# Up projection of the second sweep as seven half-width block products per pair of tiles, with its operands reread from DRAM

## The chip, the cores and the metric

The kernel runs on one core of a Trainium2 chip. The metric is the device time of one execution in microseconds. Three runs of the kernel before took 506.97, 507.06 and 507.6 us, median 507.06. One execution was profiled as well. TensorE (PE) multiplies; its weight loads are listed apart as PEld. VectorE (DVE), ScalarE (ACT) and GpSimd (POOL) do the elementwise work, and SyncE (SP) issues nearly all DMA transfers, one after the other, from one queue that also waits in order.

## The reference

One input x of 2048 rows and 512 columns feeds two branches, mixed by a gate per row. Everything is float32.

```python
g = sigmoid((x * gate_w).sum(-1, keepdims=True))
# a: linear attention, 32 heads of 16; softmax features of q and k, both signs
q, k, v = split(x @ wqkv)
phi_q, phi_k = [concat(softmax(p), softmax(-p)) for p in (q @ w_phi, k @ w_phi)]
a = ((phi_q @ (phi_k.T @ v)) / (phi_q @ phi_k.sum() + 1e-6)) @ wo
# b: feed forward, 512 -> 1792 -> 512
h = x @ w1 + b1
b = where(h > 0, h, 0) ** 2 @ w2 + b2
out = g * a + (1 - g) * b
```

## The kernel before

Every product is made from two parts of each operand, a high part (a copy rounded to the matmul's input type) and a low part (the rest): high by high, high by low, low by high. `mm3` (L73) issues these three matmuls for one pair of 128-row operands.

The feed forward is worked in two sweeps. A sweep takes seven of the fourteen tiles of 128 hidden columns; inside a sweep the loop runs over four row blocks of 512 rows of x, and inside a row block over the seven tiles. For one tile, *up* (L471) makes a bank of 128 hidden columns by 512 rows in 12 matmuls of 512 columns. ACT applies bias and relu, squares, and copies out the high part; DVE subtracts for the low part (`hidden`, L457 on). Two tiles later *down* (L486) multiplies the tile by w2 into four PSUM banks (d0 to d3, called down columns here), three matmuls of 512 columns each. The main loop (L761 on) counts these tiles as t; each t has two *steps* (2t and 2t+1), and a table filled by `at(slot, ...)` (L670) says which other work is issued in which step. The first sweep also makes keys and values and sums them up. The second sweep begins at t = 28 (step 56) and carries the query side: per 128 rows a q projection (`do_q`, 12 matmuls), the feature work on DVE, ACT and POOL, a transpose on DVE (tb), and twelve small DMAs that move its 32 x 256 blocks into phiT (`transposed`, L403). Per pair of such row chunks come the numerators (`numer`, L419, 32 small matmuls) and two applications of wo (`finish`, att). phiT has one buffer, so the transfers of a pair of chunks wait for the numerators of the pair before.

In the second sweep w1 and w2 stay in SBUF: the seven tiles of each are loaded and split once around its begin (L728 to L731), three of each in a ring (`fpool`) and four in slots of `wpool` that the first sweep no longer needs (L94). x is read back per row block, high and low parts, from a DRAM copy that the first sweep made (`x_save`, `load_x`). The up banks come from a pool of two (`ps_u`). The order of instructions on each engine is set by a scheduler from the order of the code, priorities and explicit `issue_after` ties; each engine then works its row in order.

```python
work_list = [(sw, b, i) for sw in range(2) for b in range(NB) for i in range(NFH)]
for nm, s in (("w1", 48 + 2 * i if i < NSTR else 47 + 2 * i), ("w2", 52 + 2 * i)):
```

Of the kernel before, what the change touches and what calls it, by code (L numbers as in the profile page):

```python
# [16 lines left out]
P = 128  # L17
# [14 lines left out]
FOLD_AT = 9, 3  # L32
KEPT_LATE = ("w1", 0), ("w1", 1), ("w2", 0)
SUMS = ("t1", "t2", "t15", "k2")


@with_exitstack
def tile_gated_mix(ctx: ExitStack, tc: tile.TileContext, xT, xn, wqT, wkT, wphi, wv, wo, w1, b1, w2, b2, gw, out):
# [34 lines left out]
    def mm3(o, a, b, sa, sb, first, last, **kw):  # L73
        (ah, al), (bh, bl) = a, b
        nc.tensor.matmul(o, ah[:, sa], bh[:, sb], start=first, stop=False, **kw)  # L75
        nc.tensor.matmul(o, ah[:, sa], bl[:, sb], start=False, stop=False, **kw)  # L76
        return nc.tensor.matmul(o, al[:, sa], bh[:, sb], start=False, stop=last, **kw)  # L77

    ALL = slice(0, 512)
    halves = (slice(0, 256), slice(256, 512))  # L80

# [54 lines left out]
    def x_tiles(b, k):  # L136
        return (xpool.tile([P, SB], F32R, tag="xh", name=f"xh{b}_{k}"),
                xpool.tile([P, SB], F32R, tag="xl", name=f"xl{b}_{k}"))


    def x_save(b):
# [4 lines left out]
    def load_x(b):  # L146
        xs = []
        for k in range(NK):
            xs.append(x_tiles(b, k))
            for j in range(2):  # L150
                nc.sync.dma_start(xs[k][j].bitcast(F32), xkept[b, k, j])
        return xs


    def x_fetch(b):
# [27 lines left out]
    zrow = dram.tile([2 * D], F32, name="zrow")  # L183
    xkept = dram.tile([NB, NK, 2, P, SB], F32, name="xkept")
    lkept = dram.tile([NFH, 2, P, 512], F32, name="lkept")
    kvs = const.tile([P, 2 * P], F32, name="kvs")
    nc.gpsimd.memset(kvs, 0.0)
    vext = [hold.tile([P, H * VW + 32 - VW], F32, tag="vz", name=f"vext{i}") for i in range(NV)]
# [149 lines left out]
    def project(c, xs, ws, nm):  # L338
        ps = bank(nm)
        sc = slice(c * P, (c + 1) * P)  # L340
        for k in range(NK):
            mm3(ps, xs[k], ws[k], sc, ALL, k == 0, k == NK - 1)
        return ps

    def exps(ps, tag="e"):
# [73 lines left out]
    def numer(pt):  # L419
        pss = [bank(f"num{r}") for r in range(2)]  # L420

        def mm(t, q, r):
            rows = slice(64 * r, 64 * r + 64)
            return nc.tensor.matmul(pss[r][32 * q:32 * q + 32, t * 2 * P:(t + 1) * 2 * P], kvb[rows, 4 * t + q, :],
                                    pt[rows, :, :, 4 * t + q, :].rearrange("p u r s -> p (u r) s"),
                                    start=True, stop=True, skip_group_check=True)


        todo = [(t, q, r) for t in range(2) for q in range(4) for r in range(2)]
        first = mm(*todo[0])  # L430
        with tc.issue_after(first.ins):
            second = mm(*todo[1])
        with tc.issue_after(second.ins):
            for x in todo[2:]:
                mm(*x)
        o = []
        for r in range(2):
            oh = work.tile([P, 512], F32R, tag="oh", name="oh", bufs=2)
            ol = work.tile([P, 512], F32R, tag="ol", name="ol", bufs=2)
            with tc.high_priority(offset=AHEAD):  # L440
                split(pss[r], oh, ol, nc.scalar, nc.vector)
            o.append((oh, ol))
        return o

    def attended(o, u, wos):
        ps = bank("att")
        for r in range(2):
            for t in range(2):
                mm3(ps, o[r], wos[2 * r + t], slice((2 * t + u) * P, (2 * t + u + 1) * P), ALL,
                    r + t == 0, r + t == 2)  # L450
        return ps


    def up_step(ps, k, xs, wf):
        st["up"] = mm3(ps, wf, xs[k], slice(k * P, (k + 1) * P), ALL, k == 0, k == NK - 1)

    def hidden(fc, ps, later=False):  # L457
        r = work.tile([P, SB], F32, tag="r", name="r")
        nc.scalar.activation(r, ps, AF.Relu, bias=b1c[:, fc:fc + 1])  # L459
# [4 lines left out]
        low = lambda: st.update(low=nc.vector.tensor_tensor(hl, r, hh.bitcast(F32), ALU.subtract))  # L464
        if later:
            st["rest"] = low
        else:
            low()
        return hh, hl

    def up(fc, xs, wf, later):  # L471
        ps = ps_u.tile([P, SB], F32, tag="u", name="u")
        if fc == 1 and xs is st["x", 0]:

            kk = [slice(k * P, (k + 1) * P) for k in range(NK)]
            for k in range(NK):
                for j in range(2):
                    nc.tensor.matmul(ps, wf[0][:, kk[k]], xs[k][j], start=k + j == 0, stop=False)
            for k in range(NK):
                st["up"] = nc.tensor.matmul(ps, wf[1][:, kk[k]], xs[k][0], start=False, stop=k == NK - 1)  # L480
        else:
            for k in range(NK):
                up_step(ps, k, xs, wf)
        return hidden(fc, ps, later)

    def down(t, c, dps):  # L486
        sw, b, i = work_list[t]
        end = i == NFH - 1 or t == last - 2 and c == NC - 1
        st["down"] = mm3(dps[c], hid[t], down_w[sw * NFH + i], slice(c * P, (c + 1) * P), ALL, i == 0, end)

    def do_w(src):
        st["wb"] = load_w(src)
# [10 lines left out]
    def start():  # L503
# [38 lines left out]
            do_up(1)  # L542
        raw.pop(("w1", 0))
        fetch_v()

    def do_x(b):
        st["x", b] = load_x(b - NB)

    def product(ps, p, a, op, first, last):
        b, q = divmod(p, 2)  # L550
# [119 lines left out]
    def at(slot, f, *a):  # L670
        steps.setdefault(int(slot), []).append(lambda: f(*a))
# [40 lines left out]
    for b in range(NB):  # L712
        for c in range(NC):
            s = b * SL + 2 * c if b else 7 + c
            at(s, gate_load, b * NC + c)
            at(s + 2, gate_dot, b * NC + c)
        at(b * SL + 12, gates, b)
        at(b * SL + 15, x_save, b)
# [5 lines left out]
    at(46, foldq_fetch)  # L724
    for k in range(NK):
        at(50 + k, foldq_ready, k)
    at(base + 11, do_w, wo)
    for i in range(NFH):  # L728
        for nm, s in (("w1", 48 + 2 * i if i < NSTR else 47 + 2 * i), ("w2", 52 + 2 * i)):
            at(s - 2, fetch, nm, NFH + i)  # L730
            at(s, ready, nm, NFH + i)  # L731
    at(NB * SL - 1, kv_done)


# [1 line left out]
    for p in range(NB * NC // 2):  # L736
# [9 lines left out]
    for b, slot in enumerate((46, 63, 72, 82)):  # L746
        at(slot, do_x, NB + b)
# [13 lines left out]
    for t, (sw, b, i) in enumerate(work_list):  # L761
# [3 lines left out]


        with tc.issue_after(st["down"].ins) if 0 < t <= LAG else nullcontext():
            fold("k") if t == 1 else do_up(t + LAG)
        for f in steps.get(2 * t + 1, ()):
            f()  # L770
        if i == 0:
# [100 lines left out]
```

## Time and profile before

| | |
|---|---|
| median of three runs | 507.06 us |
| the profiled execution | 506.81 us |
| its span, first to last instruction | 505.0 us |
| mean granted TensorE clock | 1.000 |
| TensorE matmul busy | 500.7 us |
| weight loads / DVE / ACT / POOL busy | 404.0 / 405.2 / 253.9 / 75.6 us |
| DMA packets moved | 84.79 MB, mean 168 GB/s |

The span is 1.8 us shorter than the execution it belongs to. Busy time of PE is the time with a matmul under way; matmuls are pipelined, so the distance between starts is what one costs, and the listed length of one is longer than that. In a line of groups the columns are line, engine, operation, output and inputs, shapes and count, then busy us and mean ns of one, then idle time before and what ended it. In a timeline line they are start, length, engine, line, operation and count.

### The profile page before, as it was taken

What the parts mean: (1) busy time and instruction counts of PE and PEld (TensorE: products, weight loads), DVE (VectorE), ACT (ScalarE), POOL (GpSimd) and SP (SyncE); (2) the same over time, 40 slices, a digit from 0 to 9 for tenths busy, and PEclk for the clock granted to TensorE, in tenths of its full rate; (3) what the DMA queues carried; (4) which work ended last, traced back from release to release, by engine and by line L of the source; (5) the groups of instructions that cost most, each with busy time, mean ns of one, the idle gap of its engine ahead of it and who ended that gap; (6) DMA issues with size and microseconds to landing.
All of it is one profiled execution on the core that took longest, in us unless ns stands there. A gap on an engine that the chain in (4) does not pass through costs nothing.

```text
span 505.0 us, 9519 instructions
## 1 busy us (share of the span) xinstructions
PE 500.7 (99%) x3616; PEld 404.0 (80%) x3616; DVE 405.2 (80%) x642; ACT 253.9 (50%) x433; POOL 75.6 (15%) x77
## 2 busy tenths in 40 slices
PE   9999999999999999999999999999999999999997
PEld 4878887788888888888888878787887878788876
DVE  4979996898877868797889898968789677798724
ACT  6598573364743646373765653443425353433530
POOL 5304020302050000000004122202122222202100
PEclk9999999999999999999999999999999999999999
DMA  8998888965657656845669161212153321032102
GB/s 296 331 361 299 232 283 270 321 234 192 212 183 245 236 165 208 279 140 155 187 183 311 51 195 52 91 51 92 39 185 96 86 74 44 8 100 82 43 22 83
DMA packets 52437, 84.79 MB, mean 168 GB/s; under 512 B 8104, under 2 KB 14504, under 8 KB 52392
## 3 DMA queue, kind: packets, MB, share of 16 engines
q1 hardware_dynamic: 52072, 83.79, 51.5%
q8 instruction: 28, 0.46, 0.4%
q10 hardware_dynamic: 288, 0.39, 0.3%
q14 instruction: 17, 0.14, 0.1%
q0 software_dynamic: 32, 0.01, 0.0%
HBM read 56.37 MB, written 21.50 MB: 154 GB/s over the span
## 4 chain that ended last, share of the span: by engine, by line
PE 97%; ACT 1%; DMA 1%; DVE 0%; issue 0%
PE d L75 10%; PE u L75 10%; PE d L77 10%; PE d L76 10%; PE u L76 10%; PE u L77 10%; PE q L75 3%; PE q L77 3%; PE att L77 3%; PE q L76 3%; PE att L76 3%; PE att L75 3%; PE ky L75 2%; PE ky L76 2%; PE ky L77 2%; PE kvps L378 2%
## 5 line engine op out<-in xcount | busy, mean ns | idle before, releaser
L459 ACT ACTIVATE r<-u,b1c 128x512 f32<-128x512 f32 x56 | 38.4, 685 | 146.1 <-PE u L77 146.0
L387 POOL TENSOR_TENSOR ez<-e,z 128x512 f32<-128x512 f32 x32 | 41.3, 1312 | 279.8 <-ACT e L358 160.5
L75 PE MATMUL d<-w2h,hh 128*128 128x512 f32 x160 | 62.7, 392 | 0.0
L77 PE MATMUL d<-w2h,hl 128*128 128x512 f32 x160 | 62.3, 389 | 0.0
L76 PE MATMUL d<-w2l,hh 128*128 128x512 f32 x160 | 62.3, 389 | 0.0
L75 PE MATMUL u<-xh,w1h 128*128 128x512 f32 x152 | 59.6, 392 | 0.1
L76 PE MATMUL u<-xl,w1h 128*128 128x512 f32 x152 | 59.2, 389 | 0.0
L77 PE MATMUL u<-xh,w1l 128*128 128x512 f32 x152 | 59.2, 389 | 0.0
L363 DVE TENSOR_REDUCE sm<-e 128x64 f32<-128x1024 f32 x32 | 38.9, 1215 | 18.5 <-ACT e L358 18.5
L464 DVE TENSOR_TENSOR hl<-r,hh 128x512 fp32r<-128x512 f32 x56 | 38.5, 687 | 13.8 <-ACT hh L463 13.7
L411 ACT ACTIVATE phiT<-tb 32x256 f32<-32x256 f32 x64 | 26.5, 413 | 32.1 <-DVE tb L405 31.4
L358 ACT ACTIVATE e<-e 128x1024 f32<-128x1024 f32 x32 | 33.8, 1056 | 11.9 <-DVE e L356 11.6
L463 ACT ACTIVATE hh<-r 128x512 fp32r<-128x512 f32 x56 | 35.3, 630 | 1.5
L460 ACT ACTIVATE r<-r 128x512 f32<-128x512 f32 x56 | 35.2, 629 | 1.3
L75 PEld LDWEIGHTS d<-w2h,hh 128*128 128x128 f32 x160 | 30.0, 188 | 6.7 <-issue 0.6
L77 PEld LDWEIGHTS d<-w2h,hl 128*128 128x128 f32 x160 | 30.0, 188 | 6.3
L76 PEld LDWEIGHTS d<-w2l,hh 128*128 128x128 f32 x160 | 30.1, 188 | 6.1
L75 PEld LDWEIGHTS u<-xh,w1h 128*128 128x128 f32 x152 | 28.5, 188 | 7.6 <-issue 0.8
L276 POOL TENSOR_TENSOR row<-xin 128x256 f32<-128x256 f32 x16 | 17.5, 1103 | 112.8 <-DVE S2ol L70 24.8
L77 PEld LDWEIGHTS u<-xh,w1l 128*128 128x128 f32 x152 | 28.5, 188 | 6.1
L76 PEld LDWEIGHTS u<-xl,w1h 128*128 128x128 f32 x152 | 28.5, 188 | 5.8
L389 DVE TENSOR_REDUCE dz<-ez 128x64 f32<-128x1024 f32 x16 | 19.4, 1210 | 9.4 <-POOL ez L387 9.3
(544 smaller groups left out, 1161.6 us busy)
## 6 DMA issues: line engine op xcount, KB each, us to landing
in<-in_w SPq DMA_DIRECT2D x66, 256.0 KB, 3.3
phiT<-tb SPq DMA_DIRECT2D x192, 32.0 KB, 1.9
w2l<-lkept SPq DMA_DIRECT2D x20, 256.0 KB, 3.7
w1l<-lkept SPq DMA_DIRECT2D x19, 256.0 KB, 4.4
xin<-in_xT SPq DMA_DIRECT2D x16, 256.0 KB, 5.0
xkept<-xh SPq DMA_DIRECT2D x16, 256.0 KB, 3.6
xkept<-xl SPq DMA_DIRECT2D x16, 256.0 KB, 4.0
in<-in_xn SPq DMA_DIRECT2D x16, 256.0 KB, 2.8
```

Of the source, the lines that this page charges most:

```text
L75: nc.tensor.matmul(o, ah[:, sa], bh[:, sb], start=first, stop=False, **kw)
L76: nc.tensor.matmul(o, ah[:, sa], bl[:, sb], start=False, stop=False, **kw)
L77: return nc.tensor.matmul(o, al[:, sa], bh[:, sb], start=False, stop=last, **kw)
L358: nc.scalar.activation(ef, ef, AF.Exp)
L363: nc.vector.tensor_reduce(sm, e3, AX.X, ALU.add)
L387: nc.gpsimd.tensor_tensor(ez[:, hs, :], e3[:, hs, :], zbc[half], ALU.mult)
L389: nc.vector.tensor_reduce(dz, ez, AX.X, ALU.add)
L411: nc.scalar.activation(dst, src, AF.Copy)
L459: nc.scalar.activation(r, ps, AF.Relu, bias=b1c[:, fc:fc + 1])
L460: nc.scalar.activation(r, r, AF.Square)
L463: st["act"] = nc.scalar.activation(hh, r, AF.Copy)
L464: low = lambda: st.update(low=nc.vector.tensor_tensor(hl, r, hh.bitcast(F32), ALU.subtract))
```

## The change

In each row block of the second sweep the first tile stays as it was. The other six are taken in pairs. A pair of tiles is a product of a 256 x 512 matrix (two tiles of w1, transposed) by a 512 x 512 matrix (x of the row block). Both are cut into two by two blocks, and the four blocks of the result are made from seven block products instead of eight (Winograd's form), each 128 hidden columns by 256 rows of x over a depth of 256: six matmuls of 256 columns.

- The sums of x that this needs (s) are made by POOL once per row block from another read of x (`s_fetch`, `s_make`), split into high and low by ACT and POOL (`s_ready`).
- The sums of w1 are made once, in row block 0, by POOL, and split by ACT and POOL (`w_fetch`, `w_sums`, `w_split`). Every operand, high part in one half and low part in the other half of a 128 x 512 tile, is stored to DRAM (`w_keep`). In row blocks 1 to 3 the 23 operand tiles (two of the single tile, seven per pair) are read back into a ring of 11 (`w_again`).
- w2 of the second sweep has only the ring of three left; its seven tiles are stored (`w2_keep`) and reread in row blocks 1 to 3 (`w2_again`).
- A pair uses two PSUM banks. One (uy) collects four products; after the first, second and third of them ACT copies it out (`snap`: v1, v2, v3). The other holds two halves (x and z). DVE adds a copy and the bias to a half (`added`). The five parts of a pair stand in the program between the down columns of one t and ahead of those of the next.
- Matmuls of the second sweep are tied into one chain in the order of the code (`in_turn`).
- In the first sweep the last row block's x is saved earlier (step 44 for 57), and the folded q weights are fetched two and split three to five steps earlier.

```diff
+W_RING = ("w1h", "w1l", "w1h", "w1l", "B210h", "B210l", "B211h", "B211l", "w1h", "w1l", "T31h")
+W_OPS = ("B11", "B21", "B22", "T1", "T3", "T2", "T4")
+NOP = 2 + NFH // 2 * len(W_OPS)
+HB = SB // 2
...
     def ffn_tiles(nm, fc):
-        if fc >= NFH + NSTR:
-            return slots(("B21", "T1", "T4", "T3")[fc - NFH - NSTR], int(nm == "w2"), f"{nm}{fc}")
...
+    def s_ready(b, k):
+        hi, lo = x_again(f"s{b}_{k}")
+        src = st["sr", b][k]
+        with tc.issue_after(st["act"].ins):
+            nc.scalar.activation(hi, src, AF.Copy)
+        nc.gpsimd.tensor_tensor(lo, src, hi.bitcast(F32), ALU.subtract)
...
+    def w_again(b, n):
+        nc.sync.dma_start(w_tile(b, n).bitcast(F32), wkept[n])
...
+    def w_split(q, op):
...
+        with tc.issue_after(st["act"].ins):
+            nc.scalar.activation(t[:, :HB], src, AF.Copy)
+        nc.gpsimd.tensor_tensor(t[:, HB:], src, t[:, :HB].bitcast(F32), ALU.subtract)
+        w_keep(n, t)
...
+    def w2_again(i):
+        t = ffn_tiles("w2", NFH + i)
+        for j in range(2):
+            nc.sync.dma_start(t[j].bitcast(F32), w2kept[i, j])
...
+    def half_product(o, b, q, a, op, first, last):
...
+        with in_turn():
+            for kk in range(2):
+                wk = w[:, kk * P:(kk + 1) * P], w[:, HB + kk * P:HB + (kk + 1) * P]
+                st["pe"] = mm3(o, wk, x[k + kk], slice(0, P), halves[h], first and kk == 0, last and kk == 1,
+                               skip_group_check=True)
...
+    def pair_part(u, part):
+        b, q = work_list[u][1], work_list[u][2] // 2
+        if part == 0:
...
+            half_product(y, b, q, "A11", "B11", True, False)
+            st["v1"] = snap("v1", "T40h", y)
+            half_product(x, b, q, "A12", "B21", True, True)
+            r = st["r0"] = work.tile([P, SB], F32, tag="r", name="r")
+            added(r[:, :HB], x, u, st["v1"])
+            nc.scalar.activation(r[:, :HB], r[:, :HB], AF.Relu)
+            return
+        y, z = st["uy"], st["uz"]
+        if part == 1:
+            half_product(y, b, q, "S2", "T2", False, False)
+            st["v2"] = snap("v2", "T40l", y)
+        elif part == 2:
+            half_product(z, b, q, "S1", "T1", True, False)
+            half_product(y, b, q, "S3", "T3", False, False)
+            v3 = snap("v3", "T41h", y)
+            r = st["r1"] = work.tile([P, SB], F32, tag="r", name="r")
+            added(r[:, HB:], z, u + 1, v3)
+        elif part == 3:
+            half_product(y, b, q, "A22", "T4", False, True)
...
+            hid[u] = squared(r)
+        else:
+            half_product(z, b, q, "S4", "B22", False, True)
+            r = st["r1"]
+            added(r[:, :HB], z, u + 1, st["v2"])
+            nc.scalar.activation(r, r, AF.Relu)
+            hid[u + 1] = squared(r)
...
+        at(55 + 2 * i, w2_keep, i)
+        for b in range(1, NB):
+            at(52 + b * SL + 2 * i, w2_again, i)
...
+    at_least = 62
+    for j in range(NOP, NB * NOP):
+        b, n = divmod(j, NOP)
+        use, free = w_slot(b, n)[0], w_slot(*divmod(j - len(W_RING), NOP))[1]
+        at_least = max(at_least, free, use - 6)
+        assert at_least <= use - 2, (b, n, at_least, use)
+        at(at_least, w_again, b, n)
...
+            elif t + LAG > last or work_list[t + LAG][0] == 0 or work_list[t + LAG][2] == 0:
+                do_up(t + LAG)
+            else:
+                pair_part(*((t + LAG, 0) if work_list[t + LAG][2] % 2 else (t + LAG - 1, 4)))
...
+                if c < NC - 1 and t + LAG <= last and work_list[t + LAG][0] and work_list[t + LAG][2] % 2:
+                    pair_part(t + LAG, c + 1)
```

More of the change, by code (lines that the diff above doesn't have):

```diff
@@ L185, in tile_gated_mix @@
     lkept = dram.tile([NFH, 2, P, 512], F32, name="lkept")
+    wkept = dram.tile([NOP, P, 512], F32, name="wkept")
+    w2kept = dram.tile([NFH, 2, P, 512], F32, name="w2kept")
     kvs = const.tile([P, 2 * P], F32, name="kvs")
@@ L446, in attended @@
         ps = bank("att")
[L447 to L450, printed above, removed]
+        with in_turn():
+            for r in range(2):
+                for t in range(2):
+                    st["pe"] = mm3(ps, o[r], wos[2 * r + t], slice((2 * t + u) * P, (2 * t + u + 1) * P), ALL,
+                                   r + t == 0, r + t == 2)
         return ps
@@ new lines, in w_tile, with w_keep, w_single @@
+    def w_tile(b, n):
+        j = b * NOP + n
+        assert j == st.get("w_n", 0)
+        st["w_n"] = j + 1
+        tag = W_RING[j % len(W_RING)]
+        t = (fpool if tag in ("w1h", "w1l") else wpool).tile([P, 512], F32R, tag=tag, name="wop")
+        w_op(b, n, t)
+        return t
+    def w_again(b, n):
+        nc.sync.dma_start(w_tile(b, n).bitcast(F32), wkept[n])
+    def w_keep(n, t):
+        nc.sync.dma_start(wkept[n], t.bitcast(F32))
+    def w_single():
+        hi, lo = w_tile(0, 0), w_tile(0, 1)
+        with tc.issue_after(st["act"].ins):
+            split(raw.pop(("w1", NFH)), hi, lo, nc.scalar, nc.vector)
+        for n, t in enumerate((hi, lo)):
+            w_keep(n, t)
@@ new lines, in w_fetch @@
+    def w_fetch(q):
+        if q < 2:
+            t = work.tile([P, 2 * D], F32, tag="tb", name="w1in", bufs=2)
+            t = t[:, :D], t[:, D:]
+        else:
+            t = [stage.tile([P, 512], F32, tag="in", name="in") for _ in range(2)]
+        for j in range(2):
+            nc.sync.dma_start(t[j], w1[NFH + 1 + 2 * q + j])
+        for j in range(2):
+            for k in range(2):
+                raw["V", q, k, j] = t[j][:, k * HB:(k + 1) * HB]
+    def w_split(q, op):
+        k, j = {"B11": (0, 0), "B21": (1, 0), "B22": (1, 1), "T1": (0, 0), "T3": (0, 1), "T2": (1, 1), "T4": (1, 0)}[op]
+        src = raw["V", q, k, j]
+        n = 2 + q * len(W_OPS) + W_OPS.index(op)
+        t = w_tile(0, n)
+        with tc.issue_after(st["act"].ins):
+            nc.scalar.activation(t[:, :HB], src, AF.Copy)
+        nc.gpsimd.tensor_tensor(t[:, HB:], src, t[:, :HB].bitcast(F32), ALU.subtract)
+        w_keep(n, t)
```

135 lines of the change are left out of this document (111 added, 24 removed).

## The prediction

> **What bounds the kernel now.** I read the page first (busy shares, the chain that ended last), then the timeline of the tail, where one row block's last products are made in 256 columns, then SyncE's (SP's) own timeline and the groups of DVE, ACT and POOL in the second sweep.
>
> ```profile
> span 505.0 us, 9519 instructions
> PE 500.7 (99%) x3616; PEld 404.0 (80%) x3616; DVE 405.2 (80%) x642; ACT 253.9 (50%) x433; POOL 75.6 (15%) x77
> PE 97%; ACT 1%; DMA 1%; DVE 0%; issue 0%
> 251.00:505.00 254.00, 250.85 (x1408) 203.00 (x1395) 198.85 (x311) 109.80 (x193) 41.30 (x32) 1.00 0.31 95
> 251.75 0.50 PE L75 MATMUL q<-wq0h,xh 128*128 128x512 f32 x1
> ```
>
> TensorE is the chain (97%), at full granted clock. The fourth line is the second sweep alone (PE, weight loads, DVE, ACT, POOL, clock, DMA share, GB/s): PE never idles, DVE is busy 199 of 254 us, the DMA engines carry 95 GB/s. So PE columns taken out are time, and every new wait of PE is time as well. What a column costs stands in the tail:
>
> ```profile
> 490.74 0.39 PE L75 MATMUL att<-wo0h,oh 128*128 128x512 f32 x1
> ...
> 500.04 0.39 PE L77 MATMUL d<-w213h,hl 128*128 128x512 f32 x1
> 500.04 0.19 PEld L75 LDWEIGHTS end<-w212h,hh 128*128 128x128 f32 x1
> 500.26 0.28 PE L75 MATMUL end<-w212h,hh 128*128 128x256 f32 x1
> ...
> 501.57 0.28 PE L77 MATMUL end<-w213h,hl 128*128 128x256 f32 x1
> ```
>
> The first two lines are the first and last of 42 matmuls of 512 columns: 9.30 us over 41 starts, 0.2268 us each (the 0.39 is a pipelined length). The last two are the first and last of 12 of 256 columns: 1.31 us over 11, 0.1191 us each, 5% more than half. The weight load of 0.19 us does not hold them up.
>
> **The change, part by part.** *Fewer columns.* A pair of up tiles was 24 matmuls of 512 columns, 5.44 us; it becomes 7 products of 6 matmuls of 256, 42 x 0.1191 = 5.00 us. Twelve pairs (3 in each of 4 row blocks) save 12 x 0.44 = **-5.3 us**. The Trainium skill ("TensorE: Matmul & The Clock Gate", "Wait — 56ns, not 53.3ns?") gives start to start as columns over 2.4 GHz plus 2.5 ns, 215.8 and 109.2 ns; by that the pair would save 0.59 us and the kernel 7.1. The trace's 227 and 119 ns carry some 10 ns more per matmul, and decide. PE's row in row block 0's second pair, after, and then the same place before (uy and uxz are the pair's two PSUM banks, s sums of x, wop a w1 operand, d a down bank, u an up bank):
>
> ```order
> L82 MATMUL uy<-s_1h,wop 128x256
> L80 MATMUL d_3562<-w2h_3319,hh 128x512
> L81 MATMUL d_3562<-w2l_3320,hh 128x512
> L82 MATMUL d_3562<-w2h_3319,hl 128x512
> L80 MATMUL uxz<-s_2h,wop 128x256
> ```
>
> ```order
> L76 MATMUL u<-xl_3_2814,w111h 128x512
> L77 MATMUL u<-xh_3_2813,w111l 128x512
> L75 MATMUL d_3451<-w2h_3355,hh 128x512
> L76 MATMUL d_3451<-w2l_3356,hh 128x512
> L77 MATMUL d_3451<-w2h_3355,hl 128x512
> ```
>
> What was one run of 12 matmuls and then four down columns has become products with a down column of three matmuls between them, their only cover while ACT and DVE read the shared banks.
>
> *Reads between products.* Three products add onto one half bank, each after ACT has copied it out.
>
> ```profile
> 384.89 0.39 PE L77 MATMUL u<-xh,w1l 128*128 128x512 f32 x1
> 385.12 0.39 PE L75 MATMUL d<-w2h,hh 128*128 128x512 f32 x1
> 385.32 0.69 ACT L459 ACTIVATE r<-u,b1c 128x512 f32<-128x512 f32 x1 [0.23 <-PE u L77]
> L67 ACT ACTIVATE oh<-num 128x512 fp32r<-128x512 f32 x16 | 8.7, 592 | 4.6 <-PE num L424 4.6
> L411 ACT ACTIVATE phiT<-tb 32x256 f32<-32x256 f32 x64 | 26.5, 413 | 32.1 <-DVE tb L405 31.4
> L358 ACT ACTIVATE e<-e 128x1024 f32<-128x1024 f32 x32 | 33.8, 1056 | 11.9 <-DVE e L356 11.6
> 501.89 0.48 DVE L817 SCALAR_TENSOR_TENSOR row<-end,rest,row 128x256 f32<-128x256 f32 x1 [0.23 <-PE end L77]
> ```
>
> ACT starts 0.20 us after PE's next slot; a copy of 256 columns lies between 413 ns (256 columns of 32 rows) and 592, I take 0.45. So 0.65 us and a wake-up, against 1.39 us of cover for the first two copies and 3 x 0.2268 = 0.68 for the third: 0 to 0.3 us per pair, and 1.06 more where an exp is ahead on ACT. I take 0.1: **+1.2** (0 to 4). DVE gets 36 additions of 0.48 us, 17 us, and loses six w1 splits: 199 becomes some 212 busy in about 250, still under PE. The first addition must pass the four reads of a q chunk before the sixth product (2.07 us of cover or more): **+1** (0 to 8, one missed down column per pair).
>
> *POOL and the first row block.*
>
> ```profile
> L276 POOL TENSOR_TENSOR row<-xin x16: 727/1046/2928, 7.9 to 146.9; 128x256 f32<-128x256 f32 x16
> L387 POOL TENSOR_TENSOR ez<-e,z x32: 1275/1292/1646, 265.2 to 468.1; 128x512 f32<-128x512 f32 x32
> L464 DVE TENSOR_TENSOR hl<-r,hh x56: 622/681/1225, 11.7 to 489.0; 128x512 fp32r<-128x512 f32 x56
> ```
>
> (Nanoseconds min/median/max.) POOL gets 81 operations: 65 of 128x256 at about 1.0 us and 16 of 512 columns at 1.29, 86 us. It does 41 now and would be half busy. Only in block 0, where the w1 operands are made, is it dense: 41 x 1.0 and 12 x 1.29 (four splits, eight ez) are 56 us in about 61; ACT's splits wait for POOL's sums there, with copies queued behind. **+2** (0 to 8).
>
> *SP: 164 more DMAs on one queue* (23 w1 and 14 w2 tiles kept, 69 and 42 reread, 16 rows of x).
>
> ```profile
> 299.88 15.10 SPq L413 DMA_DIRECT2D phiT<-tb  x24
> 371.17 0.53 SPq L151 DMA_DIRECT2D xh<-xkept  x1
> ...
> 374.90 0.32 SPq L151 DMA_DIRECT2D xl<-xkept  x1
> L413 SPq DMA_DIRECT2D phiT<-tb x192: 507/589/1698, 278.4 to 484.3; - x192
> DMA to landing us min/median/max: 2.6/4.4/6.1
> 352.80 1.09 PE L424 MATMUL num<-phiT,kvb 64*32 64x256 f32 x32
> 354.05 1.15 SPq L413 DMA_DIRECT2D phiT<-tb  x2
> SPq L413 <- PE num L424: 19.0, 4, 4.8
> SPq L413 <- DVE tb L405: 22.6, 9, 7.8
> ```
>
> SP needs 15.10/24 = 0.63 us for each small phiT transfer and 3.73/7 = 0.53 for a 256 KB one (eight in a row, 371.17 to 374.90). The landing line is that of w1's low parts, reread from DRAM: median 4.4 us. phiT has one buffer, so the 24 transfers of a chunk pair wait for the numerator matmuls of the pair before (num at 352.80, first transfer at 354.05; the last two lines are SP's waits for it and for DVE's transpose: total, times, longest). From 252 us on SP issues 192 phiT and 56 others (24 of x, 16 loads of partial results, 16 stores): 192 x 0.63 + 56 x 0.53 = 151 us; with some 150 of the new ones 231 us, in the 245 us that PE would need. A queue that full, in order, with waits in it, comes late. The Trainium skill ("DMA: Bandwidth & Descriptors", "Issuing engines are not separate DMA queues") says the sequencer's time to start a DMA is usually small relative to the DMA itself. By that this part costs 0 and the sum is about 506. Here 0.59 us of issue stands against some 4 of landing and, for phiT, takes half of SP: the rows decide.
>
> SP's row around the second chunk pair's transfers, which follow the first pair's numerators, before and then after (wop from wkept is a reread w1 operand, w2kept a store of w2):
>
> ```order
> L413 DMA phiT<-tb 32x256 x24
> L824 DMA out<-row 128x512 x2
> L810 DMA row<-part 128x512 x2
> L413 DMA phiT<-tb 32x256 x24
> L661 DMA out<-row 128x512
> ```
>
> ```order
> L545 DMA wop<-wkept 128x512 x4
> L449 DMA phiT<-tb 32x256 x12
> L586 DMA w2kept<-w2h_3698 128x512
> L586 DMA w2kept<-w2l_3699 128x512
> L545 DMA wop<-wkept 128x512 x2
> L449 DMA phiT<-tb 32x256 x12
> L586 DMA w2kept<-w2h_3771 128x512
> L586 DMA w2kept<-w2l_3772 128x512
> L545 DMA wop<-wkept 128x512 x3
> ```
>
> Where two transfers of results stood between bursts, rereads now do, with stores of w2 ahead of them. The tiles come as single high, single low, B11, B21; B22, T1; T3, T2, T4. So T2 of block 1's first pair stands behind 24 phiT and 7 others. Count from the start of the numerators: 1.25 + 24 x 0.63 + 7 x 0.53 + 4.4 = 24.5 us to its landing. PE gets to it after the numerators (1.09), one up tile, four down columns, att, q, att and a down column (63 matmuls of 512, 14.3) and two products (1.43): 16.8 us. **+7.7** (shortest rows 0.507, 0.32 and 2.6 give +1.5; landing 6.1 and a transpose 3 us late, within the 7.8 above, give +12.4). At the next burst one reread stands between the twelves and T2 right behind them: 1.25 + 24 x 0.63 + 0.53 + 4.4 = 21.3 us against 24.5 of PE's work, 3.2 us early, unless the transpose is that late. I take **+3** for the five middle bursts (0 to 25, five like the last). The last burst is like the first; SP's row, before and after:
>
> ```order
> L656 DMA row<-part 128x512
> L661 DMA out<-row 128x512
> L413 DMA phiT<-tb 32x256 x24
> L824 DMA out<-row 128x512 x3
> L820 DMA out<-row 128x256
> ```
>
> ```order
> L591 DMA w2l_6176<-w2kept 128x512
> L591 DMA w2h_6175<-w2kept 128x512
> L449 DMA phiT<-tb 32x256 x24
> L545 DMA wop<-wkept 128x512
> L591 DMA w2h_6232<-w2kept 128x512
> ```
>
> A reread now waits behind the burst where only stores did. That one wop is the last T4: 1.25 + 15.1 + 4.4 = 20.8 us after the numerators start, and PE wants it after 1.09 + 14.5 = 15.6: **+5.2** (0.4 to 10).
>
> *The rest* (earlier saves and folds in sweep one, SP about two thirds free there) I cost at nothing; its cover is SP's free time before 252 us.
>
> **Sum.** -5.3 + 1.2 + 1 + 2 + 7.7 + 3 + 5.2 = +14.8 us on the profiled execution's 506.8 (span 505.0): 521.6. The median of the runs is 507.06, 0.25 higher; I say **521.5**.
>
> **Rivals.**
> 1. *The rereads land in time, and it is faster.* Place: T2 and T4 above. The sum is 506.8 - 5.3 + 2 = **503.5**. It needs SP's lateness under 3 us in all: T2's margin would need about 0.3 us per phiT issue, and the shortest row is 0.507; or PE already held elsewhere in the gap. For it: ring and steps give each tile at least two steps (two times 245/56 us) of lead. It is the case of the skill's rule above. 0.16.
> 2. *Landing grows.* Traffic in the sweep goes from 95 GB/s to about 250 (150 x 0.262 MB more in 254 us). In the program each DMA of SP waits for the one eight before it, so above 8 x 0.53 = 4.3 us of landing SP slows further: at 6.1 us it issues one per 0.76, 217 x 0.23 = 50 us more, 281 us of SP against 245: 506.8 - 5.3 + 36 = **537.5**, and the wait may feed itself. 0.12.
> 3. *POOL or ACT in block 0 is the bound and SP is not*: all their upper ends and no SP term, 506.8 - 5.3 + 8 + 4 + 1 = **514.5**. The skill ("SBUF — State Buffer", "SBUF: two separate sides") has POOL and a DVE operation with two inputs lock each other out for a whole instruction; here POOL's 727 ns at best and 2928 at worst would fit, DVE's median of 681 over 622 hardly. 0.10.
>
> **How the numbers follow.** SP late: 0.62, its own range 511 to 534 (the two priced stalls at their low or high ends). Below 505 lies most of rival 1 (0.13), above 545 the worse part of rival 2 (0.06): range 505 to 545. About 1 us (0.2%) is what a measurement tells here: faster 0.15, same 0.04, slower 0.81.
>
> **What would show it.** Right: 256-column matmuls 0.119 us apart; SP issuing nearly without a gap through the second sweep; PE's waits there ending on wop, the longest near the first and the last reread. Wrong: PE waits ending on ACT's copies or on POOL's low parts instead; phiT issues well below 0.5 us; or a busy PE and a shorter sweep, which is rival 1.

## The result, and the profile after

The changed kernel takes 580.92 us (median of four runs, 580.53 to 581.85) against 507.15 us for the kernel before (four runs, 506.97 to 507.6): a ratio of 1.146, 95% interval 1.144 to 1.148. The forecast was 521.5 us, range 505 to 545. Slower was right; the size was not. All profiles below are of one execution each; that of the changed kernel has a span of 578.8 us.

The page, the chain of work that ended last, and the second sweep in one row (PE, weight loads, DVE, ACT, POOL, granted clock, DMA share, GB/s):

```profile
PE 512.8 (89%) x3832; PEld 416.4 (72%) x3832; DVE 431.3 (75%) x672; ACT 280.6 (48%) x512; POOL 154.5 (27%) x158
PE 62%; DMA 11%; SPq 10%; DVE 7%; issue 4%; POOL 3%; ACT 2%; POOLq 0%; ACTq 0%; DVEq 0%
251.00:578.80 327.80, 262.68 (x1633) 215.70 (x1622) 225.08 (x347) 134.78 (x266) 96.00 (x90) 0.92 0.59 194
```

Up to 250 us PE is busy for 249 us in both kernels. Over the span its time outside matmuls goes from 505.0 - 500.7 = 4.3 us to 578.8 - 512.8 = 66.0, 61.7 of the 73.8 us. The other 12.1 are busy time, although PE has fewer columns to do; the clock has fallen to 0.92. TensorE is 62% of the chain now, for 97%.

What PE waits for, the first five lines (total, times, longest):

```profile
PE att L80 <- DVE row L833: 29.3, 2, 15.9
PE u L80 <- DMA wop<-wkept: 10.1, 1, 10.1
PE uxz L80 <- DVE r L621: 10.1, 8, 4.0
PE uy L80 <- ACT v L616: 4.6, 3, 1.7
PE uy L80 <- DMA wop<-wkept: 3.9, 1, 3.9
```

Only 14.0 us end on a reread operand (wop). The longest two end on `row`: DVE's addition of the attention product to the partial result of the first sweep (part), which frees the PSUM bank. SP's timeline around them (first the kernel before, then the changed one):

```profile
265.95 0.51 SPq L656 DMA_DIRECT2D row<-part  x1
275.39 0.42 SPq L656 DMA_DIRECT2D row<-part  x1
278.39 15.47 SPq L413 DMA_DIRECT2D phiT<-tb  x24
```

```profile
286.23 16.19 SPq L449 DMA_DIRECT2D phiT<-tb  x24
306.95 3.09 SPq L169 DMA_DIRECT2D row<-in_xT  x4
310.61 3.05 SPq L545 DMA_DIRECT2D wop<-wkept  x4
324.54 8.16 SPq L449 DMA_DIRECT2D phiT<-tb  x12
342.06 0.32 SPq L830 DMA_DIRECT2D row<-part  x1
```

Before, the first partial results were fetched ahead of the first phiT burst (the first and the last of six loads are shown). Now the burst comes 8 us later and the first partial result at 342.06, behind two bursts and the rereads. PE had stood from 332.14 to 348.04.

The stops cost more than their length. PE's timeline at the 10.1 us stop, its first matmul and two later ones, and ten us at each of the two longest stops, where the granted clock is 0.53 and 0.52:

```profile
317.48 0.77 PE L80 MATMUL u<-x_0h,wop 128*128 128x512 f32 x1 [10.14 <-DMA wop<-wkept]
...
321.03 0.63 PE L82 MATMUL u<-x_2h,wop 128*128 128x512 f32 x1
321.46 0.59 PE L80 MATMUL u<-x_3h,wop 128*128 128x512 f32 x1
```

```profile
335.00:345.00 10.00, 0.00 (x0) 0.00 (x0) 5.84 (x9) 0.00 (x0) 1.88 (x2) 0.53 1.00 332
475.00:485.00 10.00, 0.00 (x0) 0.00 (x0) 7.75 (x12) 3.87 (x6) 4.93 (x4) 0.52 0.83 275
```

After the stop a matmul of 512 columns starts every 0.43 us, for some 4 us, where it was 0.227. Summed over the starts of the second sweep that waited for nothing (what lies more than 0.02 us above 0.2268 us for 512 columns or above 0.1191 for 256), slow matmuls cost 14.7 us here and 1.9 before. The Trainium skill ("TensorE: Matmul & The Clock Gate", "Wait — 56ns, not 53.3ns?") gives 426.7 ns from start to start for 512 columns in its cold state; the rows agree.

### The profile page after: what moved, and what is told of

Its sections match the earlier page's. It is cut to its first block, busy times and chain, and to the rows that moved or that the text cites. A ratio compares the mean times of both kernels' runs of the same rounds, so it can differ in the third digit from the quotient of the medians.

```text
span 578.8 us, 10474 instructions
## 1 busy us (share of the span) xinstructions
PE 512.8 (89%) x3832; PEld 416.4 (72%) x3832; DVE 431.3 (75%) x672; ACT 280.6 (48%) x512; POOL 154.5 (27%) x158
## 4 chain that ended last, share of the span: by engine, by line
PE 62%; DMA 11%; SPq 10%; DVE 7%; issue 4%; POOL 3%; ACT 2%; POOLq 0%; ACTq 0%; DVEq 0%
SPq L449 6%; PE d L80 6%; PE d L81 6%; PE d L82 6%; DMA wop<-wkept 5%; PE u L80 4%; PE u L82 4%; PE u L81 4%; PE att L80 2%; PE att L81 2%; PE att L82 2%; PE ky L80 2%; PE ky L81 2%; DMA row<-part 2%; PE ky L82 2%
## 5 line engine op out<-in xcount | busy, mean ns | idle before, releaser
L80 PE MATMUL d<-w2h,hh 128*128 128x512 f32 x222 | 87.8, 395 | 0.0
L81 PE MATMUL d<-w2l,hh 128*128 128x512 f32 x222 | 87.1, 392 | 0.0
L82 PE MATMUL d<-w2h,hl 128*128 128x512 f32 x222 | 86.7, 391 | 0.0
L497 ACT ACTIVATE r<-u,b1c 128x512 f32<-128x512 f32 x32 | 21.9, 684 | 91.9 <-PE u L82 91.8
L177 POOL TENSOR_TENSOR row<-row 128x256 f32<-128x256 f32 x32 | 26.0, 821 | 92.8 <-DMA row<-in_xT 84.2
L616 ACT ACTIVATE v<-uy 128x256 f32<-128x256 f32 x36 | 13.8, 382 | 65.0 <-PE uy L82 65.0
L80 PE MATMUL u<-xh,w1h 128*128 128x512 f32 x104 | 40.6, 390 | 0.1
L81 PE MATMUL u<-xl,w1h 128*128 128x512 f32 x104 | 40.5, 390 | 0.0
L82 PE MATMUL u<-xh,w1l 128*128 128x512 f32 x104 | 40.5, 389 | 0.0
L502 DVE TENSOR_TENSOR hl<-r,hh 128x512 fp32r<-128x512 f32 x32 | 23.5, 734 | 10.5 <-ACT hh L501 10.5
L425 DVE TENSOR_REDUCE dz<-ez 128x64 f32<-128x1024 f32 x16 | 19.4, 1215 | 14.6 <-POOL ez L423 14.6
```

Source lines behind the costliest of these rows:

```text
L177: nc.gpsimd.tensor_tensor(o, x, y, op)
L425: nc.vector.tensor_reduce(dz, ez, AX.X, ALU.add)
```

## The experiments

Each kernel was timed beside the kernel before on the same chip, which took 507.1 to 507.9 us (medians).

| run | what | us | ratio to before, 95% |
|---|---|---|---|
| no_reread | changed, no rereads | 551.9 | 1.085 to 1.092 |
| reread_act | changed, rereads from ACT's queue | 568.3 | 1.118 to 1.122 |
| before_in_turn | before, PE tied in code order | 507.6 | 0.9998 to 1.0017 |
| before_stores | before, 164 idle stores on SP | 509.9 | 1.004 to 1.008 |
| nr_no_s | no_reread, no sums of x after block 0 | 543.9 | 1.068 to 1.075 |
| nr_no_bank | no_reread, half banks not read in between | 546.6 | 1.072 to 1.079 |
| nr_no_make | no_reread, operands not made (21 stand-in loads on SP) | 551.2 | 1.083 to 1.088 |
| nr_none | all three | 526.6 | 1.034 to 1.038 |
| nr_none_act | all three, stand-in loads from ACT's queue | 517.3 | 1.015 to 1.023 |
| put_bank | nr_none_act with bank reads back | 528.6 | 1.041 to 1.047 |
| put_make | nr_none_act with making back | 538.0 | 1.059 to 1.063 |
| part_early | changed, partial results loaded early | 589.6 | 1.156 to 1.166 |
| z_late | changed, z's first product later | 582.2 | 1.143 to 1.149 |
| phi_act | changed, phiT from ACT's queue | 608.0 | 1.190 to 1.199 |
| phi_dram | changed, phiT through DRAM | 577.5 | 1.133 to 1.141 |
| combo2 | reread_act + part_early + z_late | 559.6 | 1.098 to 1.104 |
| combo3 | combo2 + phi_dram | 547.3 | 1.072 to 1.085 |
| combo3_sp | combo3, rereads on SP | 571.4 | 1.124 to 1.128 |

### Is it the rereads, SP's load, or the pairing?

```diff
 def w_again(b, n):                        # no_reread
-    nc.sync.dma_start(w_tile(b, n).bitcast(F32), wkept[n])
+    w_op(b, n, st["ring"][(b * NOP + n) % len(W_RING)])
...
-    nc.sync.dma_start(w_tile(b, n).bitcast(F32), wkept[n])
+    nc.scalar.dma_start(w_tile(b, n).bitcast(F32), wkept[n])   # reread_act; w2_again likewise
...
+    spare = dram.tile([164, P, 512], F32, name="spare")        # before_stores
+    def spare_store():
+        n = st["spare"] = st.get("spare", -1) + 1
+        nc.sync.dma_start(spare[n], b2b)
...
+    with in_turn():                                            # before_in_turn, round each product
```

> The 111 rereads of w1 operands and w2 in row blocks 1 to 3 are left out: the tiles that row block 0 left in the rings are used again, so the output is not the reference's from row 512 on; pairing, sums, copies, the stores to DRAM and the ties of TensorE's order stay. Theory Q (SP's one in-order queue, loaded with the rereads, brings operands and partial results late): nearly all of the 74 us goes, 505 to 515 us (the prediction's own terms without SP: 506). Theory P (the pairing itself: half-bank reads by ACT and DVE, POOL's sums and splits in row block 0, the tied order): most of it stays, 550 us or more. Theory D (the DMA engines are full, whoever issues): as Q, 505 to 515.

> The 111 rereads are issued from ACT's queue instead of SP's, everything else as in the changed kernel. Theory Q: they no longer stand behind the phiT bursts, 510 to 535 us; TensorE's waits on wop and on the rows of partial results shrink from 50 us to under 15. Theory D: the same bytes through the same DMA engines, 565 us or more. Theory P: no change, 575 to 585. If ACT, held by waits of its own DMAs, becomes late with exponentials and squares instead, 535 to 565 with TensorE waiting for ACT or DVE.

> The kernel before with 164 stores of one constant 256 KB tile to DRAM on SP, in the steps in which the changed kernel has its stores, rereads and second loads of x; nobody waits for what they move. Theory Q in its strong form (the load on SP alone delays phiT and the rows of partial results until TensorE stops): 520 to 550 us. Theory Q in its weak form (it is the rereads' own late data that stops TensorE): 507 to 515. Theory P: 507 to 510.

> The kernel before with only the ties that put TensorE's matmuls of the second sweep in the order of the code. Theories Q and D: 506 to 509 us. Theory P, as far as the tied order is its cause: 515 us or more.

Theory Q fell in its strong form: without a single reread the kernel still takes 551.9 us, 45 over before. The rereads are worth 29.0 us, and issued from ACT they give back 12.7. That 568.3 us is what theory D expected of full DMA engines (565 or more), but D's number for no_reread (505 to 515) failed with Q's. Nor is it SP's issue time by itself: 164 transfers more on SP cost the kernel before 2.8 us. PE's tied order costs the kernel before nothing. PE's waits without rereads:

```profile
PE att L80 <- DVE row L831: 16.0, 1, 16.0
PE uxz L80 <- DVE r L619: 13.2, 8, 4.0
PE uy L80 <- ACT v L614: 4.5, 3, 1.8
```

Both waits for wop are gone and the second wait of att with them (13.4 us in the changed kernel). The first is there as long as ever, so it is no reread that it stands behind.

### What of the pairing costs the 45 us?

```diff
 def s_fetch(b):                           # nr_no_s; s_make and s_ready likewise,
+    if b: return                          # x stands in for s
...
-            nc.scalar.activation(t, ps, AF.Copy)               # nr_no_bank: snap, and
+            nc.scalar.activation(t, b2b[:, :HB], AF.Copy)      # two of the additions
...
 def w_split(q, op):                       # nr_no_make: no w_fetch, no w_sums
+    nc.sync.dma_start(w_tile(0, n).bitcast(F32), xkept[0, n % 4, n // 4 % 2])
```

> As the kernel without rereads (551.9 us), and in row blocks 1 to 3 the sums of x are not fetched, made or split; the block's x tiles stand in for them, so the output is not the reference's from row 512 on. Theory S (the rows of x for the sums come late behind phiT on SP; POOL, then ACT, then DVE wait for them in order, and with DVE the additions to att): the 16.0 us wait of att goes, and with it a clock dip, 528 to 536 us. Theory B (half-bank reads are the main loss): the wait of att stays in some other place, 545 to 553. Theory M (making w1's operands in row block 0 is the main loss and everything later follows from it): 545 to 553.

> As the kernel without rereads (551.9 us), and ACT's three copies and DVE's additions to the x half and to the first z product read a constant tile instead of the half banks, so that TensorE never waits for a reader between the products of a pair; the output of the second sweep's feed forward is not the reference's. Theory B: TensorE's waits on r (13.2 us) and v (4.5 us) go, and DVE and ACT are no longer held by TensorE: 525 to 534 us. Theories S and M: only those 18 us at most, and the 16.0 us wait of att stays: 534 to 545.

> As the kernel without rereads (551.9 us), and the 21 operands of the pairs are loaded in row block 0 by one transfer each from stored x instead of being summed and split by POOL and ACT and stored; the output of the second sweep's feed forward is not the reference's. Theory M: the waits of row block 0 (7.5 us up to 296 us) go and the later ones shrink too, 530 to 540 us. Theories S and B: only the waits of row block 0 go, 542 to 548.

> All of the above left out together: no rereads, no sums of x after row block 0, no reads of half banks between products, no making of operands; the output is not the reference's. What is left of the change is TensorE's pattern: seven products of 256 columns for a pair, 5.3 us less than before by the prediction's rows. If that gain is real: 500 to 506 us. If the pattern itself (256 columns, a fixed order, downs in between) costs time: 510 us or more.

Taken out one at a time they give 8.0, 5.3 and 0.7 us, taken out together 25.3. None of S, B and M has it alone, and all three ranges for the main loss were missed. In nr_no_s the wait of att is 11.5 us for 16.0, in nr_no_bank 14.6, and in nr_no_make 10.9 with 7.2 more ahead of it. In nr_none the largest wait was of the experiment's own making: a stand-in operand 10.3 us late behind a phiT burst on SP. The stand-in loads were moved to ACT's queue, which gave 9.3 us back, and then one part at a time was put back. nr_no_make has the same 21 loads on SP, so its 0.7 us is not the price of the making.

> The run with everything left out (526.6 us), with the 21 stand-in loads of row block 0 issued from ACT's queue, so that none stands behind a phiT burst. Its waits were 17.0 us and slow matmuls behind them some 5; 10.3 and 2.5 of these were the stand-in loads'. If that is so and TensorE's pattern has the predicted gain: 508 to 515 us. If the pattern is slower by itself: 520 or more.

> The run with everything left out (517.3 us), with the copies and additions reading the half banks again: no rereads, no sums of x after row block 0, no making of operands. By the prediction's terms (1.2 and 1 us): 518 to 521 us. By the waits that it showed in the kernel without rereads (13.2 us on r, 4.5 on v, and the clock behind them): 530 to 538.

> The run with everything left out (517.3 us), with the operands made by POOL and ACT in row block 0 and stored again: no rereads, no sums of x after row block 0, no reads of half banks. By the prediction's term (2 us, at most 8): 518 to 525. If making delays the features of row block 0, and with them the first phiT bursts and the partial results behind them on SP: 528 to 540, with a wait of att at the start of row block 1.

nr_none_act still has TensorE's pattern, the copies and additions on ACT and DVE (of other tiles), the sums of x of row block 0, the stores of w2 and the stand-in loads. It takes 10 us more than before (517.3, a little above what was expected). What PE still waits for there, and the second sweep in one row:

```profile
PE kvps L422 <- DVE e L413: 4.5, 1, 4.5
PE att L80 <- DVE ol L75: 3.6, 2, 2.2
PE num L468 <- issue: 1.7, 1, 1.7
251.00:516.10 265.10, 251.49 (x1665) 211.63 (x1664) 215.61 (x349) 123.95 (x243) 44.59 (x35) 0.98 0.35 111
```

Put back alone, the bank reads cost 11.3 us (528.6, between the two ranges expected) and the making of the operands 20.7 (538.0, in the range of late partial results). With both put back the kernel is nr_no_s: 543.9, so together they cost 26.6 and not 32.0. The prices of parts put back singly do not add up either: 5.4 us are counted in both. The sums of x of blocks 1 to 3 cost the same wherever they are added, 8.0 us from nr_no_s to no_reread and 8.6 from put_make to nr_no_bank. From before up, the 73.8 us are 10.2 for what nr_none_act has, 26.6, 8.0, and 29.0 for the rereads.

The waits of PE that the bank reads bring in put_bank are for the read of the x half (r) and ACT's copies (v), 12.4 us (the wait of kvps, 5.4, is in nr_none_act too):

```profile
PE uxz L80 <- DVE r L610: 8.3, 7, 2.0
PE uy L80 <- ACT v L605: 4.1, 4, 2.0
```

Five of the seven waits on r are at the first product of z (0.25 to 2.04 us, all in blocks 1 to 3). It writes the other half of the bank from which DVE still has to read x, and it is released by that read. No run shows whether the chip needs this wait or only the program asks for it.

PE's waits in put_make, and then SP's timeline there, after that of nr_none_act:

```profile
PE att L80 <- DVE row L839: 11.5, 2, 11.3
PE att L80 <- DVE ol L75: 4.2, 2, 2.7
PE num L468 <- DMA wkept<-wop: 4.1, 1, 4.1
PE uy L82 <- POOL wop L585: 2.0, 1, 2.0
```

```profile
262.35 1.48 SPq L803 DMA_DIRECT2D z<-zrow  x2
271.37 0.32 SPq L819 DMA_DIRECT2D row<-part  x1
283.84 16.78 SPq L457 DMA_DIRECT2D phiT<-tb  x24
```

```profile
266.03 0.98 SPq L1041 DMA_DIRECT2D part<-row  x2
268.09 2.10 SPq L820 DMA_DIRECT2D z<-zrow  x2
282.55 4.21 SPq L557 DMA_DIRECT2D wkept<-wop  x3
288.12 15.57 SPq L457 DMA_DIRECT2D phiT<-tb  x24
330.94 1.06 SPq L836 DMA_DIRECT2D row<-part  x2
```

With the making back, the load of the first partial result goes from 271.37 to 330.94, from ahead of the first burst to behind the second (48 transfers), and the wait of att is back. SP holds stores of operands there that POOL has yet to write (three take 4.21 us), but the burst itself starts when DVE's first transpose has ended, at 288.09, 4.3 us later than in nr_none_act. On POOL the first weighting by z (ez) of the second sweep is later too (nr_none_act, then put_make):

```profile
267.18 1.28 POOL L431 TENSOR_TENSOR ez<-e,z 128x512 f32<-128x512 f32 x1 [11.95 <-PE uxz L82]
```

```profile
267.35 2.13 POOL L585 TENSOR_TENSOR wop<-w1in,wop 128x256 fp32r<-128x256 f32 x3 [6.89 <-ACT wop L584]
273.55 2.75 POOL L431 TENSOR_TENSOR ez<-e,z 128x512 f32<-128x512 f32 x2 [4.07 <-DVE r L627]
```

ez stands in POOL's row behind operands that wait for ACT, but that is not what holds it. POOL is idle for 4.07 us ahead of it, and it starts 0.13 us after the landing of its z (273.42; 267.02 in nr_none_act); the view names the DVE instruction that ended last before it. SP issues the load of z at 268.09 for 262.35, behind two stores of partial results that wait for DVE. In the changed kernel z lands at 270.13, as POOL comes free, and ez starts at 270.37. On ez wait the features, the transposes and the burst: DVE stands 2.44 us for it in put_make.

The making is not the only thing that puts the partial results behind the bursts. In nr_no_make, where no operand is made, the first is loaded at 332.61, behind two bursts as well. Of the kernels without rereads only nr_none_act and put_bank load it ahead of the first burst.

### Does it help to make what is late early?

```diff
+        at(t - 10, part_load, n)                       # part_early; s rows in the idle "in" ring
...
-            half_product(z, b, q, "S1", "T1", True, False)   # z_late: from part 2 ...
+            half_product(z, b, q, "S1", "T1", True, False)   # ... to the end of part 3
...
-                    nc.sync.dma_start(dst, src)
+                    nc.scalar.dma_start(dst, src)            # phi_act
...
+        nc.sync.dma_start(phid[n], tb)                       # phi_dram, in place of 12 + 4 copies
+        for j in range(4):
+            nc.sync.dma_start(pt[32 * j:32 * j + 32, u, :, :, :].rearrange("p r g s -> p r (g s)"),
+                              phid[n].rearrange("(r i) c -> i r c", i=32)[:, :, 256 * j:256 * j + 256])
```

> The changed kernel (580.9 us) with the loads of the partial results issued ten steps ahead of the attention product that they are added to, and with the rows of x for the sums of blocks 1 to 3 in a ring that is idle there, so that a buffer for them is free. Theory Q1 (the two waits of att, 15.9 and 13.4 us, are partial results that stand behind phiT and rereads on SP): both go with their clock dips, 546 to 556 us. Theory V (DVE, held by its own chain of features and transposes, makes the addition late whenever its row lands): att still waits 10 us or more in all, 563 to 576 us.

> The changed kernel with the first product of the z half moved from before the third down column to after it, so that DVE has one product and one down column more to read the x half of the same bank. Theory B1 (TensorE's waits on r are the read of the x half, and nothing else is behind them): the 10.1 us of waits on r fall under 3, and with the clock 568 to 573 us. If the time they cost is only handed on to the next late load: 576 to 582 us.

> The changed kernel with the 192 small phiT transfers issued from ACT's queue. Theory Q: SP loses 122 us of issue; the waits of TensorE on rereads and partial results go, 535 to 550 us. If the issue time stops ACT instead (0.6 us each, 7.6 us for a chunk, ahead of copies and squares): 560 to 600 us, TensorE waiting on v and r.

> The changed kernel with each chunk's phiT moved through DRAM: one store of the transposed tile and four reads of 32 x 1024 in place of twelve transfers of 32 x 256 and four copies on ACT, 80 issues on SP for 192 and 64 ACT copies fewer, at one more landing (about 3 us) for each chunk. Theory Q (SP's issue time in the bursts is what makes rereads and partial results late): 535 to 555 us, TensorE's waits on wop and on the rows of partial results under 20 us in all. If the landing of a chunk counts and not the issue: 575 to 595.

None of the four helps alone. part_early takes the waits of att away, and the time goes up by 8.7 us, above both ranges expected, because the wait moves:

```profile
PE uy L80 <- DMA wop<-wkept: 40.4, 6, 18.8
PE u L80 <- DMA wop<-wkept: 10.1, 1, 10.1
```

Not a microsecond is left on att's rows and 50.5 us are on rereads: whatever stands first on SP, the rest is late. z_late changes next to nothing (+1.3). The waits on r fall from 10.1 to 4.7 us, and PE waits 9.3 us for a reread at a place where it had not. phi_act moves the issue time with the transfers: PE's waits on ACT's copies go to 42.2 us, the longest 17.7, and 27 us are lost, more than either range had. phi_dram has 80 issues for 192 and gains 3.4 us: theory Q's number (535 to 555) is refuted, and the rival's (575 to 595, a landing more per chunk) came true. Its waits for partial results are even longer, 35.7 us in three. So it is not the number of issues in the bursts. SP's longest total of waits there is for DVE's transposes:

```profile
SPq L443 <- DVE tb L442: 71.1, 13, 8.5
```

What PE needs stands in one row with transfers that wait for DVE. That this, and not the landing more, keeps phi_dram slow is not shown by itself.

> Rereads issued from ACT, partial results loaded ten steps ahead, sums' rows in the idle ring, and the z half's first product late, all together. If the waits are each other's equals and independent: 568 less 16.7 (att) less some 12 (r) less the clock dips behind them, 532 to 542 us. If each wait hides another: 550 us or more. Under 507 would take every other wait away too, and is not expected.

> phiT through DRAM, rereads issued from ACT, partial results loaded early, sums' rows in the idle ring, the z half's first product late. Without the last change of phiT it took 559.6 us, with waits for ACT's copies (some 15 us), DVE (12) and w2 (6). If ACT's 64 copies (26.5 us) and SP's bursts were behind them: 528 to 542 us. If it is DVE's and POOL's chain of features: 550 to 560.

> The same with the rereads left on SP. Theory Q with SP relieved of 112 issues: no dearer than from ACT, 525 to 540 us. If a reread must not stand behind anything that waits: 545 to 565, TensorE waiting on wop.

combo2 (559.6 us) came out as if each wait hid another. combo3 (547.3) lies between its two ranges, combo3_sp (571.4) above both of its own. These two differ only in the queue of the rereads, and by 24.1 us. On SP they leave PE waiting for wop, as in the last line; from ACT no such wait of any length is left (the first three):

```profile
PE uy L80 <- ACT v L613: 7.2, 7, 3.2
PE num L457 <- DMA phiT<-phid: 6.8, 3, 4.4
PE uxz L80 <- DVE r L618: 4.8, 3, 3.5
```

```profile
PE uy L80 <- DMA wop<-wkept: 31.8, 5, 13.9
```

The Trainium skill ("DMA: Bandwidth & Descriptors", "Issuing engines are not separate DMA queues") says that starting DMAs from several engines saves only the sequencer's time. For time of issue alone before_stores bears that out (2.8 us for 164 transfers). For a queue that waits in order it does not: here the other queue is worth 24.1 us.

combo3 is the best version of the change that computes the whole reference: 547.3 us, 33.6 less than the changed kernel and 39.9 more than the kernel before. No run that keeps the change beats the kernel before.

## Why the prediction was wrong in size

The working gave -5.3 for columns and +20.1 for all waits. Measured, the waits and the slow matmuls behind them are nearly four times that. The step that failed worst is the term for POOL and the first row block; the other terms for waits were too small as well, and two parts had none. By its steps:

- *Fewer columns, -5.3.* The spacing held: in the changed kernel twelve matmuls of 256 columns run from 258.35 to 259.65, 0.118 us each.

```profile
258.35 0.28 PE L80 MATMUL uy<-x_0h,wop 128*128 128x256 f32 x1
...
259.65 0.28 PE L82 MATMUL uxz<-x_3h,wop 128*128 128x256 f32 x1
```

  In nr_none_act, though, PE is busy 501.6 us for 500.7 before, and slow matmuls explain 2.7 of that (4.6 for 1.9). So some 1.8 us of gain are seen. Over the undisturbed starts of the second sweep the spacing of 512 columns was 0.2286 us there (734 starts) for 0.2269 before (1,032), another 1.2 us; the 57 that follow a matmul of 256 columns had 0.2335. The rest is open.
- *Reads between products, +1.2 and +1.* Failed in size: 11.3 us put back alone, near the sum of both upper ends (12), and 5.9 on top of the making. The cover of 2.07 us was counted right. The addition to x misses it in five of twelve pairs, by up to 2.04 us, and ACT's copies miss theirs four times, by 4.1 us in all where 0.1 per pair was taken.
- *POOL and the first row block, +2 (0 to 8).* Failed: 20.7 us put back alone, 15.3 on top of the bank reads. It weighed POOL's busy time (56 of 61 us) and the wait for the operands themselves, which is small indeed (2.0 us on wop). It left out SP. With the making, the load of z comes 5.7 us later and the first burst 4.3 us, the partial results are loaded behind two bursts, and PE waits 11.3 us for the first of them.
- *SP, +7.7, +3 and +5.2.* Rereads cost 29.0 us for 15.9; they are 29.0 of 73.8 us, where the prediction had 15.9 of its 20.1 there. The mechanism was right, its places only in part. The last T4 came 3.9 us late (5.2 forecast). T2 of block 1's first pair, the dearest term, was not waited for at all. The single tile's operands ahead of it were 10.1 us late, with 14 other transfers between the burst and the first of them, and then PE stood for att until 348.04, when T2 had landed (338.04). The partial results behind the rereads were not priced: +3 for the middle bursts stands against a 13.4 us wait of att.
- *The sums of x of row blocks 1 to 3.* The sum has no term for them; it took POOL as dense in block 0 alone. They cost 8.0 to 8.6 us.
- *The rest, at nothing.* Its cover, SP's free time before 252 us, was there. But in nr_none_act PE waits 4.5 us on a DVE that is full at the start of the sweep (9.8 of 10 us from 250 to 260, for 8.2 before), and the kernel ends 10 us above before.
- *Not in the sum:* the clock, 12.8 us (14.7 for 1.9).

Of the rivals, the first (rereads land in time) fell; its rule on issue time held only where nobody waits. The second (landing grows) is not separated: the median landing of a reread w1 operand was 5.0 us for the 4.4 assumed, and the DMA engines were full in stretches (share 1.00 at 332 GB/s from 335 to 345 us), while PE stood. The third had a right place, the making in row block 0, at 13 us at most with its other terms, and was given 0.10; but it had the time on POOL and ACT and none on SP, where put_make's longest wait comes from. What was to be seen if right was seen in part: SP has hardly a gap from 286 to 340 us and wop is waited for, but the longest waits end on partial results. The signs named for wrong, waits on ACT's copies and DVE's reads, were there beside them.

What stays open: what holds combo3 at 40 us over before (its waits of more than 0.8 us come to 21.6 us and its slow matmuls to 12.3), and why the order of SP puts the partial results behind the bursts wherever operands or sums of x are made; the traces show that it does.

## What to carry to other kernels

Price a moved or added operation by what stands behind it in its queue, engine by engine, up to the engine that is the bound, and not by the busy time that it adds. Where PE is 97% of the chain, a long stop can count twice, once as a wait and once as slow matmuls (10.1 us, and 2.1 behind it). Parts of a change hide behind each other: here neither the prices of parts taken out singly nor those of parts put back singly add up. So time the pairs too, and see that a stand-in does not bring a wait of its own.

## What the runs showed of the hardware

A stop of some 2 us can slow the clock, and need not. In nr_none the 2.22 us below came ahead of a slow stretch: from the sixth matmul after the stop on, seven follow 0.43 us apart (378.22 to 381.20), at a granted clock of 0.67 from 377 to 380 us. In nr_none_act a stop of 2.23 us at the same place in the program (the last line) had none behind it, and the clock stayed at 1.00 from 369 to 376 us.

```profile
376.86 0.50 PE L80 MATMUL att<-wo0h,oh 128*128 128x512 f32 x1 [2.22 <-DVE ol L75]
...
378.64 0.63 PE L80 MATMUL att<-wot,oh 128*128 128x512 f32 x1
379.07 0.63 PE L81 MATMUL att<-wot,oh 128*128 128x512 f32 x1
```

```profile
369.74 0.50 PE L80 MATMUL att<-wo0h,oh 128*128 128x512 f32 x1 [2.23 <-DVE ol L75]
```

The slowing came 1.4 us after PE was back at work. Behind stops of 1.7 to 2.9 us the slow matmuls cost from 0.1 us (put_bank, a stop of 1.73 us) to 2.8 (no_reread, 2.83 us). The Trainium skill ("TensorE: Matmul & The Clock Gate", "What's actually happening") has the clock fall after an idle window of some 3.4 us that runs freely. The stop of 2.22 us is shorter than that, and what one window counts no run here shows.
